# Down weights of units 2 to 7 fetched as whole words and split on chip, and the last two divisions later

## The chip, the cores and the metric

One core of a Trainium2 chip (trn2) runs the whole kernel in one launch; inputs and output are in HBM, all tensors FP32. The metric is the device time of one execution in microseconds. The engines are TensorE (PE in the profile; PEld is its weight load), VectorE (DVE), ScalarE (ACT), GpSimd (POOL) and SyncE (SP), which only issues transfers. POOL also issues some; those of SP and POOL run on the same 16 DMA engines.

## The reference

Linear attention over 8 batches x 8 heads (576 tokens, head size 64, 128 random features), and then a two-layer block on the 4608 tokens x 512 features that it gives.

```python
def phi(x):
    proj = np.einsum('bhsd,df->bhsf', x, w_phi)
    proj = proj - np.max(np.abs(proj), axis=-1, keepdims=True)
    return np.concatenate([np.exp(proj), np.exp(-proj)], axis=-1)
q_p, k_p = phi(q), phi(k)
kv, z = np.einsum('bhsf,bhsd->bhfd', k_p, v), np.sum(k_p, axis=2)
num = np.einsum('bhsf,bhfd->bhsd', q_p, kv)
den = np.einsum('bhsf,bhf->bhs', q_p, z)[..., None] + 1e-06
attn = num / den
...
h = x @ w_in
g = np.maximum(h, 0.0) + alpha * np.minimum(h, 0.0)
return g @ w_out
```

Here x is attn with heads side by side, w_in is 512 x 2048 and w_out 2048 x 512.

## The kernel before, in words

**Attention, 0 to about 320 us.** 32 pairs of heads are worked through one slot after another (`attention_units`); the table in `places` says at which slot each part of pair i comes. Near the end of a pair the denominator goes out to DRAM and comes back inverted and spread over partitions (`rec_out`, `spread`, L528 and L533), POOL multiplies the numerator by it (`finish`, L538: the division), and SP stores the product to `x_d` (L541). In between, the 64-bit weights are decoded to FP32 halves and stored twice: as whole words in `a_d` (256 columns per quarter, one word each), and as two parts, high and low, in `u_d` (up weights) and `v_d` (down weights). Every FP32 product is three matmuls: high x high, low x high, high x low (L584 to L586, L594 to L596, L876 to L878).

**Chunk 0, about 320 to 400 us.** The first 512 tokens go through the block plainly. The 2048 hidden features are 16 groups, ff = 0 to 15; two groups are a unit u. `up2` makes h of a group (12 matmuls), ACT and DVE turn it into g and split it (relu r, join g L265, cast gh, rest gl L152), and `down2` adds its product to the outputs po (12 matmuls, called d0 to d15 here). The order on PE is up 0 to 3, d0 to d3, up 4, up 5, then d4, up 6, d5, up 7 and so on to d13, up 15; then the first product of pair 1, d14, another product, d15. A slot of this order is U2 = 1/3 in the table's time, with t1 = 33.051 at d0. The weights come by SP: wa and ws for up, and `load_down` (L648) fetches wd of group ff + 4 when d of ff has been issued, so that d4 to d15 take theirs from `v_d`; the first four were kept on chip.

**Sums, beside chunk 0 and the first units.** The 4096 tokens that remain go as 4 pairs of chunks, by a scheme with 7 products in place of 8 that needs sums of weight quarters. `sums(u, down)` makes them: load the unit's whole words from `a_d` (POOL's queue, L713), two and then two more subtractions or additions (L720 to L727), split into high and low (halve on ACT L146, low on DVE L149), store to `us_d` or `vs_d` (POOL's queue, L741). They are needed for all 8 down units and all 8 up units; those of up units 3 to 7 are made just in time, in the units. SUMS lists them in order; the first NSUM = 9 (up and down of units 0 to 2, down of 3 to 5) are placed in chunk 0, one each 3 slots (SUM0, SUMD, with SUMT for the parts), the rest in the units of pair 1, in a `for` over u at the end. In chunk 0 the tiles of the sums come from rings: 3 for the loaded words, 4 for the split sums, so that a new split waits for an older store.

**Pair 1 and after.** `unit(p, u)` makes the 7 up products of a unit (6 matmuls each) into banks pa, pb, pc, and `down_pair` the down products.

PE, SP and POOL (and in attention ACT and DVE) follow the order of the table `todo`, sorted by time. From T2 on the order of ACT and DVE is set by the scheduler, in which `behind` keeps splits and sums behind the newest cast and rest. Each engine then works strictly in its order.

Of the kernel before, what the change touches and what calls it, by code (L numbers as in the profile page):

```python
# [26 lines left out]
NF = DFF // P  # L27
# [13 lines left out]
NPRE = 2  # L41
# [19 lines left out]
def places(i):  # L61
    early = True
    end = i >= NPAIR - 2
    lag = 0 if i >= NPAIR - 4 else 1
    first = {}
    if i == 0:
        first = dict(
            kz=0.5093, ka=0.6934, ko=0.8124, kr=1.1197, kc=1.4241,
            n=1.8361, q=(0.96, 0.9362, 0.4904), qe=(0.9994, 1.0, 0.8939),
        )  # L70
    if i == 1:
        first = dict(kz=0.0015, ka=0.0046, ko=0.0058)
    return dict(
        ld=-2.1 if i > 2 else -1.9,
        lv=-0.17 if i > 2 else -0.45,
        p=(-0.9955 if early else -0.997, -0.2197),
        pl=-0.219 if i > 2 else -0.2217,
        ke=(0.005, 0.008) if i > 2 else (-0.1643, -0.0202),
        kz=1.0035,
        ka=1.0012,  # L80
        ko=1.0045,
        kr=1.0191,
        kc=1.1461,
        q=(1.4089, 1.4543, 1.3558),
        qe=(1.4364, 1.4627, 1.3892),
        d=2.004,
        ds=2.0047,
        n=2.0062,
        s=2.1311,
        d9=2.025,  # L90
        dv=lag + 2.7686 if early else 2.842 if end else 2.7432,
        rd=lag + 2.82,
        rr=lag + 3.03 if lag else 3.06,
        x=lag + 3.72,
        xs=lag + 4.05 if lag else 3.851,
        y=0.0055,
        s0=2.007,
    ) | first
# [3 lines left out]
W0 = dict(load=-1.3, scale=-1.0712, split=-0.9512)  # L102
X0T = 5.52
X0L = 0.305
WDT = (33.2, 33.83, 33.86)
HEADS = (31.9, 32.3, 32.62, 32.9)
T2 = 33.05
HEAD = 4
# [1 line left out]
U2 = 1 / 3  # L110
# [1 line left out]
PAD = 32  # L112
GQ = (0.1093, 0.2682, 0.3222)
UPA = 2
SUM0, SUMD = 1.5, 3.0
SUMT = dict(load=-5.0, two=0.0, four=0.2, half0=0.6, half1=0.8, store0=1.5, store1=1.6)
SUMS = [(0, 0), (0, 1), (1, 0), (1, 1), (2, 0), (2, 1), (3, 1), (4, 1), (5, 1), (6, 1), (7, 1)]
NSUM = 9
NJIT = 3
XPT = (19.3, 19.301, 20.3, 21.3, 22.3, 31.7, 32.1, 32.4)  # L120
XP0, XPD = 6.6, 2.0
# [3 lines left out]
def fused_kernel(ctx: ExitStack, tc: tile.TileContext, kq, v, w_phi, w_in, w_out, alpha, out):  # L125
    nc = tc.nc
# [10 lines left out]
    def f(t):  # L137
        return t.bitcast(F32)
# [6 lines left out]
    def halve(dst, src):  # L145
        return act.activation(dst, src, AF.Copy, scale=0.5)  # L146

    def half_low(dst, src, hi):
        return dve.scalar_tensor_tensor(dst, src, 0.5, f(hi), op0=ALU.mult, op1=ALU.subtract)  # L149
# [79 lines left out]
    def decode_store(ff, z, o, n):  # L229
# [8 lines left out]
        load=decode_load,  # L238
# [14 lines left out]
    def behind(eng):  # L253
        return tc.issue_after(newest[eng].ins) if eng in newest and "pso" in late else ExitStack()
# [346 lines left out]
    xs, po = {}, {}  # L601
# [43 lines left out]
    def down_tile(name, dtype):  # L645
        return wdq.tile([P, 2, 2, WN], dtype, tag="wd", name=name, bufs=2 * NPRE)

    def load_down(ff):  # L648
        u, r = divmod(ff, 2)
        wd[ff] = down_tile(f"wd{ff}", F32R)  # L650
        nc.sync.dma_start(f(wd[ff]), v_d[u, :, 2 * r : 2 * r + 2])

    def load_up(p, u):
        if p:
# [42 lines left out]
    def sums(u, down):  # L697
# [13 lines left out]
        def load():  # L711
# [2 lines left out]
            st["b"] = [a[:, n] for n in ((0, 2, 1, 3) if down else (A11, A12, A21, A22))]  # L714
            st["src"] = (a[:, 0:2], a[:, 2:4]) if down else (a[:, 1:3], a[:, 0:4:3])

        def two():
            a11, a12, a21, a22 = st["b"]
            with behind("dve"):
                dve.tensor_tensor(a22, a21, a22, op=ALU.add)  # L720
                dve.tensor_tensor(a21, a11, a21, op=ALU.subtract)
# [7 lines left out]
        def half(n):  # L729
            a = st["src"][n]  # L730
            t = st[n] = new(n + 1).bitcast(F32R).rearrange("p (n t c) -> p n t c", t=2, c=WN)
            with behind("act"):
                halve(t[:, :, 0], a)
            with behind("dve"):
                half_low(t[:, :, 1], a, t[:, :, 0])
            if "hv" in late and not down:
                for j, s in enumerate(((S1, S2), (S3, S4))[n]):
                    wu[1, u, s] = t[:, j]
# [2 lines left out]
            pool.dma_start((us_d, vs_d)[down][u, :, 2 * n : 2 * n + 2], f(st[n]))  # L741

        parts = dict(load=load, two=two, four=four)
        parts |= {f"half{n}": lambda n=n: half(n) for n in range(2)}
        return parts | {f"store{n}": lambda n=n: store(n) for n in range(2)}

# [98 lines left out]
    for n, (k, ff) in enumerate(order):  # L845
        t = HEADS[n] if n < HEAD else t1 + (n - HEAD) * U2
        if k == "d":
            todo.append((t, lambda ff=ff: down2(ff)))
            if ff + 2 * NPRE < NF:
                todo.append((max(t + 0.0005, (WDT + (0,) * NF)[ff]), lambda ff=ff + 2 * NPRE: load_down(ff)))  # L850
            continue
        todo.append((t, lambda ff=ff: up2(0, ff)))
        if n >= HEAD and ff % 2 and ff // 2 + UPA < NU:
            todo.append((t + 0.0006, lambda u=ff // 2 + UPA: load_up(0, u)))
        for i, dt in enumerate(GH.get(ff, (0, *GQ))):
            todo.append((t + U2 - 0.01 + dt, lambda ff=ff, i=i: glu2(0, ff, i)))
    for u in range(NOWN, HEAD // 2 + UPA):
        todo.append((t1 + 0.0001 + 2.5 * U2 * (u > NOWN), lambda u=u: load_up(0, u)))
    work = [sums(*x) for x in SUMS] + [sums(u, 0) for u in range(NJIT, NU)]
    for n, parts in enumerate(work[:NSUM]):  # L860
        for k, dt in SUMT.items():
            todo.append((max(t1 + 0.0002, t1 + (SUM0 + SUMD * n + dt) * U2 + 0.002), parts[k]))
    for n, t in enumerate(XPT + tuple(t1 + (XP0 + XPD * n) * U2 + 0.003 for n in range(11))):
        todo.append((t, lambda n=n: (prep.extend(prepare(1) if n == 0 else []), pieces(1))))
    todo.append((t1 + 5 * U2, lambda: prep.pop(4)()))
# [279 lines left out]
```

## Time and profile before

| | |
|---|---|
| runs | 1002.67, 1003.82, 1003.88 us, median 1003.82 |
| profiled execution | 1001.65 us, span 999.9 us, granted clock 0.998 |
| PE matmul busy | 976.2 us (98%), 7200 instructions |
| DVE, ACT, POOL busy | 744.1 us (74%), 625.5 us (63%), 242.2 us (24%) |
| DMA | 258.52 MB, mean 259 GB/s |

The busy share is an average over stages with different limits. The page has a row of 40 slices for each engine, the DMA engines and the granted clock; views with a window show one stretch. A timeline gives, for each instruction, how long its engine was idle before it and who ended that; a view of waits sums this by pairs. Most rows of a helper (halve, low) have the helper's line, so tiles tell them apart: sv and su are tiles of sums of down and up weights, xo and xr inputs of pair 1 and later.

### The profile page before, as it was taken

The numbers are of one execution on the slowest core, as the hardware profiler recorded it, in microseconds if no ns is written. First come the engines' busy times: TensorE is split into PE (matmuls) and PEld (weight loads), VectorE is DVE, ScalarE is ACT, GpSimd is POOL, SyncE is SP. The second block draws the span as 40 slices with busy tenths as digits, with TensorE's granted clock in tenths as the row PEclk, the third lists the DMA queues.
The fourth block names the chain that finished last, engine by engine and source line by source line (L and its number), as shares of the span: only waits on it lengthen the run. The fifth ranks groups of instructions, "written<-read, shape, count | busy, mean of one in ns | idle before, by whom it ended". The sixth has DMA issues, their size and how long they took to land.

```text
span 999.9 us, 19129 instructions
## 1 busy us (share of the span) xinstructions
PE 976.2 (98%) x7200; PEld 789.5 (79%) x7200; DVE 744.1 (74%) x1174; ACT 625.5 (63%) x1224; POOL 242.2 (24%) x218
## 2 busy tenths in 40 slices
PE   8999999999999999899999999999999999999998
PEld 7666666666666877787888888888888888888887
DVE  6888888888885577687997465888366977565874
ACT  4799899899898234455566454665455655554553
POOL 1466676666665131121000000000000000000001
PEclk9999999999999999999999999999999999999999
DMA  5588889999885999996767566768567677565565
GB/s 180 186 297 289 301 300 310 313 316 328 310 278 195 333 352 417 378 330 215 275 215 276 183 238 204 273 209 275 202 208 250 234 238 265 169 221 192 185 221 182
DMA packets 99339, 258.52 MB, mean 259 GB/s; under 512 B 12656, under 2 KB 13296, under 8 KB 99248
## 3 DMA queue, kind: packets, MB, share of 16 engines
q1 hardware_dynamic: 88816, 221.71, 65.5%
q0 software_dynamic: 10000, 35.39, 9.2%
q8 instruction: 57, 0.93, 0.4%
q14 instruction: 34, 0.28, 0.1%
q10 hardware_dynamic: 432, 0.20, 0.1%
HBM read 196.16 MB, written 60.96 MB: 257 GB/s over the span
## 4 chain that ended last, share of the span: by engine, by line
PE 58%; DMA 9%; DVE 3%; issue 3%; ACT 1%; POOL 1%; SPq 0%; ACTq 0%; DVEq 0%; POOLq 0%
PE pa L876 5%; PE pa L878 5%; PE pa L877 5%; PE qa L878 5%; PE qa L877 5%; PE qa L876 5%; PE pc L876 3%; PE pc L877 3%; PE pc L878 3%; DMA xr<-x_d 2%; DMA sv<-a_d 2%; PE qc L878 2%; DMA vs_d<-sv 2%; PE qc L877 2%; PE qc L876 2%
## 5 line engine op out<-in xcount | busy, mean ns | idle before, releaser
L142 ACT CAST hv<-g 128x512 fp32r<-128x512 f32 x224 | 135.4, 618 | 80.8 <-PE qa L878 44.3
L152 DVE TENSOR_TENSOR hv<-g,hv 128x512 fp32r<-128x512 f32 x224 | 150.3, 685 | 40.4 <-ACT hv L142 39.1
L766 POOL DMA_DIRECT2D out_dram<-pt x35 | 19.0, 543 | 503.3 <-ACT pt L1044 419.0
L354 DVE TENSOR_REDUCE m<-pj 128x8 f32<-128x1024 f32 (+2 forms) x67 | 78.5, 1172 | 36.1 <-PE pj L350 36.1
L878 PE MATMUL qa<-hv,wv 128*128 128x512 f32 (+1 forms) x257 | 97.3, 379 | 0.1
L877 PE MATMUL qa<-hv,wv 128*128 128x512 f32 (+1 forms) x257 | 97.2, 378 | 0.0
L876 PE MATMUL qa<-hv,wv 128*128 128x512 f32 (+1 forms) x257 | 97.2, 378 | 0.0
L355 DVE TENSOR_TENSOR t<-pj,m 128x1024 f32<-128x1024 f32 (+2 forms) x67 | 78.8, 1177 | 4.4
L350 PE MATMUL pj<-w_sb,raw 64*128 64x128 f32 x1024 | 75.3, 287 | 4.1 <-DVE t L355 4.1
L350 PEld LDWEIGHTS pj<-w_sb,raw 64*128 64x128 f32 x1024 | 63.2, 189 | 19.5 <-issue 15.3
L377 POOL TENSOR_TENSOR y<-xk 128x1024 f32<-128x1024 f32 x30 | 71.0, 2368 | 5.2 <-ACT xk L369 5.2
L488 PE MATMUL n<-qf,sf 128*64 128x288 f32 x512 | 69.2, 412 | 0.0
L204 POOL TENSOR_TENSOR aw<-cw,aw 128x512 int32<-128x512 int32 x32 | 41.7, 1302 | 110.6 <-DVE aw L200 92.0
L369 ACT ACTIVATE xk<-t 128x1024 f32<-128x1024 f32 (+1 forms) x66 | 64.1, 1022 | 5.0 <-DVE t L355 5.0
L896 ACT ACTIVATE r<-g 128x512 f32<-128x512 f32 x65 | 37.4, 622 | 46.9 <-DVE g L892 46.8
L390 PE MATMUL kv<-xk,v 128*64 128x256 f32 x512 | 62.3, 385 | 0.0
L477 ACT ACTIVATE qf<-qt 128x512 f32<-128x512 f32 x116 | 60.8, 648 | 0.0
L142 ACT CAST xo<-xr 128x512 fp32r<-128x512 f32 x56 | 33.6, 619 | 43.4 <-DVE xr L819 21.9
L897 DVE SCALAR_TENSOR_TENSOR g<-r,al,g 128x512 f32<-128x512 f32 x65 | 45.9, 747 | 17.1 <-ACT r L896 16.9
L878 PEld LDWEIGHTS qa<-hv,wv 128*128 128x128 f32 x257 | 48.6, 189 | 7.3 <-DVE hv L152 0.5
L152 DVE TENSOR_TENSOR xo<-xr,xo 128x512 fp32r<-128x512 f32 x56 | 38.7, 701 | 20.8 <-ACT xo L142 20.4
L876 PEld LDWEIGHTS qa<-hv,wv 128*128 128x128 f32 x257 | 48.6, 189 | 6.9
(203 smaller groups left out, 2534.3 us busy)
## 6 DMA issues: line engine op xcount, KB each, us to landing
wv<-vs_d SPq DMA_DIRECT2D x64, 512.0 KB, 4.3
ws<-us_d SPq DMA_DIRECT2D x54, 512.0 KB, 3.8
wv<-v_d SPq DMA_DIRECT2D x48, 512.0 KB, 5.9
wa<-u_d SPq DMA_DIRECT2D x37, 512.0 KB, 5.5
raw<-kq_dram SPq DMA_DIRECT2D x31, 576.0 KB, 6.7
v<-v_dram SPq DMA_DIRECT2D x32, 320.0 KB, 5.1
rr<-rec_d SPq DMA_DIRECT2D x64, 144.0 KB, 3.8
x_d<-rr SPq DMA_DIRECT2D x32, 288.0 KB, 3.6
```

The lines of the kernel that those rows point to most:

```text
L142: return act.copy(dst, src)
L152: return eng.tensor_tensor(dst, src, f(hi), op=ALU.subtract)
L350: pe.matmul(dst[h, j], lhsT=c["raw"][hs, ts], rhs=w_sb[hs], start=True, stop=True)
L354: dve.tensor_reduce(m, src, axis=AX.X, op=ALU.max, apply_absolute_value=True)
L355: dve.tensor_tensor(t[:, hs, js], src, m.unsqueeze(3).broadcast_to([P, nh, nj, FD]), op=ALU.subtract)
L369: act.activation(x[:, a, :, js], c["t", 0][:, :, js], AF.Exp, scale=sg)
L377: pool.tensor_tensor(y, x[:, :, : 2 * FD], x[:, :, 2 * FD :], op=ALU.add)
L390: pe.matmul(c["kv"][h * D : (h + 1) * D, 0:2], lhsT=c["v"][:, tp, h, :], rhs=c["x", ch][:, :, h, j, :], start=tp == 0, stop=tp == NV - 1,)
L488: pe.matmul(ps[h * D : (h + 1) * D, :], lhsT=c["st"][:, a, h * D : (h + 1) * D], rhs=c["qf"][:, h, a, u * HS : (u + 1) * HS], start=a == 0 ...
L876: pe.matmul(ps, lhsT=wh, rhs=xh, start=first, stop=False, skip_group_check=True)
L877: pe.matmul(ps, lhsT=wl, rhs=xh, start=False, stop=False, skip_group_check=True)
L878: pe.matmul(ps, lhsT=wh, rhs=xl, start=False, stop=end, skip_group_check=True)
```

## The change

Three things. `load_down` is gone: `split_down` makes wd of groups 4 to 15 from the words of the sums' load, by a halve on ACT and a low on DVE for each group, in two new parts split0 and split1 of `sums`, ahead of the additions, which overwrite the words. The order of the sums follows: down units 2 to 7 each one to two slots before the d that needs its parts, up units 0 to 2 between, and down units 0 and 1, whose parts are on chip, in the units of pair 1. And for the last two pairs of heads the division and its store move from slot 3.72 and 3.851 to 6.75 and 6.76.

```diff
--- before.py
+++ after.py
@@ -91,8 +91,8 @@
         dv=lag + 2.7686 if early else 2.842 if end else 2.7432,
         rd=lag + 2.82,
         rr=lag + 3.03 if lag else 3.06,
-        x=lag + 3.72,
-        xs=lag + 4.05 if lag else 3.851,
+        x=lag + 3.72 if not end else 6.75,
+        xs=lag + 4.05 if lag else 6.76 if end else 3.851,
         y=0.0055,
         s0=2.007,
     ) | first
@@ -102,7 +102,6 @@
 W0 = dict(load=-1.3, scale=-1.0712, split=-0.9512)
 X0T = 5.52
 X0L = 0.305
-WDT = (33.2, 33.83, 33.86)
 HEADS = (31.9, 32.3, 32.62, 32.9)
 T2 = 33.05
 HEAD = 4
@@ -112,10 +111,10 @@
 PAD = 32
 GQ = (0.1093, 0.2682, 0.3222)
 UPA = 2
-SUM0, SUMD = 1.5, 3.0
-SUMT = dict(load=-5.0, two=0.0, four=0.2, half0=0.6, half1=0.8, store0=1.5, store1=1.6)
-SUMS = [(0, 0), (0, 1), (1, 0), (1, 1), (2, 0), (2, 1), (3, 1), (4, 1), (5, 1), (6, 1), (7, 1)]
-NSUM = 9
+SUMT = dict(load=-5.0, split0=-1.3, split1=-1.1, two=0.0, four=0.2, half0=0.6, half1=0.8, store0=1.5, store1=1.6)
+SUMS = {(2, 1): 5.4, (0, 0): 7.4, (3, 1): 9.4, (4, 1): 13.4, (1, 0): 15.4, (5, 1): 17.4, (6, 1): 21.4, (2, 0): 23.4, (7, 1): 25.4}
+NSUM = len(SUMS)
+SUMS |= {(u, 1): None for u in range(NPRE)}
 NJIT = 3
 XPT = (19.3, 19.301, 20.3, 21.3, 22.3, 31.7, 32.1, 32.4)
 XP0, XPD = 6.6, 2.0
@@ -645,10 +644,12 @@
     def down_tile(name, dtype):
         return wdq.tile([P, 2, 2, WN], dtype, tag="wd", name=name, bufs=2 * NPRE)
 
-    def load_down(ff):
-        u, r = divmod(ff, 2)
+    def split_down(ff, a):
         wd[ff] = down_tile(f"wd{ff}", F32R)
-        nc.sync.dma_start(f(wd[ff]), v_d[u, :, 2 * r : 2 * r + 2])
+        with behind("act"):
+            halve(wd[ff][:, :, 0], a)
+        with behind("dve"):
+            half_low(wd[ff][:, :, 1], a, wd[ff][:, :, 0])
 
     def load_up(p, u):
         if p:
@@ -714,6 +715,9 @@
             st["b"] = [a[:, n] for n in ((0, 2, 1, 3) if down else (A11, A12, A21, A22))]
             st["src"] = (a[:, 0:2], a[:, 2:4]) if down else (a[:, 1:3], a[:, 0:4:3])
 
+        def split(r):
+            split_down(2 * u + r, st["src"][r])
+
         def two():
             a11, a12, a21, a22 = st["b"]
             with behind("dve"):
@@ -741,6 +745,7 @@
             pool.dma_start((us_d, vs_d)[down][u, :, 2 * n : 2 * n + 2], f(st[n]))
 
         parts = dict(load=load, two=two, four=four)
+        parts |= {f"split{n}": lambda n=n: split(n) for n in range(2)}
         parts |= {f"half{n}": lambda n=n: half(n) for n in range(2)}
         return parts | {f"store{n}": lambda n=n: store(n) for n in range(2)}
 
@@ -846,8 +851,6 @@
         t = HEADS[n] if n < HEAD else t1 + (n - HEAD) * U2
         if k == "d":
             todo.append((t, lambda ff=ff: down2(ff)))
-            if ff + 2 * NPRE < NF:
-                todo.append((max(t + 0.0005, (WDT + (0,) * NF)[ff]), lambda ff=ff + 2 * NPRE: load_down(ff)))
             continue
         todo.append((t, lambda ff=ff: up2(0, ff)))
         if n >= HEAD and ff % 2 and ff // 2 + UPA < NU:
@@ -857,9 +860,10 @@
     for u in range(NOWN, HEAD // 2 + UPA):
         todo.append((t1 + 0.0001 + 2.5 * U2 * (u > NOWN), lambda u=u: load_up(0, u)))
     work = [sums(*x) for x in SUMS] + [sums(u, 0) for u in range(NJIT, NU)]
-    for n, parts in enumerate(work[:NSUM]):
+    for (x, t), parts in zip(SUMS.items(), work[:NSUM]):
         for k, dt in SUMT.items():
-            todo.append((max(t1 + 0.0002, t1 + (SUM0 + SUMD * n + dt) * U2 + 0.002), parts[k]))
+            if x[1] or "split" not in k:
+                todo.append((max(t1 + 0.0002, t1 + (t + dt) * U2 + 0.002), parts[k]))
     for n, t in enumerate(XPT + tuple(t1 + (XP0 + XPD * n) * U2 + 0.003 for n in range(11))):
         todo.append((t, lambda n=n: (prep.extend(prepare(1) if n == 0 else []), pieces(1))))
     todo.append((t1 + 5 * U2, lambda: prep.pop(4)()))
```

Line numbers of the changed kernel are up to 5 higher in these parts, and one lower above. On POOL, where the sums' loads begin (sv_0_0 is the loaded words of the down sums of unit 0, su of up sums, rr30 the division of pair 30), before:

```order
L713 DMA su_0_0_5210<-a_d_63 128x1024
L713 DMA sv_0_0_5212<-a_d_63 128x1024
L538 TENSOR_TENSOR rr30_5216<-s30_5024,rr30_5216 128x576
L713 DMA su_1_0_5277<-a_d_63 128x1024
L741 DMA us_d_60<-su_0_1_5264 128x1024
L741 DMA us_d_60<-su_0_2_5268 128x1024
L801 DMA xr1_1_5330<-x_d_57 128x1024
L538 TENSOR_TENSOR rr31_5294<-s31_5158,rr31_5294 128x576
L713 DMA sv_1_0_5346<-a_d_63 128x1024
L741 DMA vs_d_62<-sv_0_1_5337 128x1024
```

and now, behind the loads of sv_2_0, su_0_0 and sv_3_0, which open the list one after another:

```order
L806 DMA xr1_1_5310<-x_d_57 128x1024
L745 DMA vs_d_62<-sv_2_1_5340 128x1024
L745 DMA vs_d_62<-sv_2_2_5343 128x1024
L714 DMA sv_4_0_5402<-a_d_63 128x1024
L745 DMA us_d_60<-su_0_1_5388 128x1024
L745 DMA us_d_60<-su_0_2_5394 128x1024
L714 DMA su_1_0_5457<-a_d_63 128x1024
L745 DMA vs_d_62<-sv_3_1_5449 128x1024
L745 DMA vs_d_62<-sv_3_2_5452 128x1024
L537 TENSOR_TENSOR rr30_5212<-s30_5024,rr30_5212 128x576
L714 DMA sv_5_0_5506<-a_d_63 128x1024
L537 TENSOR_TENSOR rr31_5271<-s31_5158,rr31_5271 128x576
```

The two divisions have moved behind the stores of the sums of down unit 3, and behind five and six loads of words in place of two and three.

On ACT, from the last copy of attention to the cast of group 5 (r2_0_4 and gh2_0_4 are relu and cast of group 4, wd4 the high part of the down weights of group 4), before:

```order
L500 COPY s31_5158<-n31_1_5153 128x288
L146 ACTIVATE su_0_1_5264<-su_0_0_5210 128x2x256
L146 ACTIVATE su_0_2_5268<-su_0_0_5210 128x2x256
L146 ACTIVATE sv_0_1_5337<-sv_0_0_5212 128x2x256
L146 ACTIVATE sv_0_2_5342<-sv_0_0_5212 128x2x256
L261 ACTIVATE r2_0_4_5315<-h2_0_4_5298 128x512
L142 CAST gh2_0_4_5348<-g2_0_4_5340 128x512
L142 CAST xo1_7_0_5372<-xr1_0_3099 128x512
```

and now:

```order
L499 COPY s31_5158<-n31_1_5153 128x288
L145 ACTIVATE wd4_5287<-sv_2_0_5216 128x2x256
L145 ACTIVATE wd5_5290<-sv_2_0_5216 128x2x256
L260 ACTIVATE r2_0_4_5295<-h2_0_4_5274 128x512
L141 CAST gh2_0_4_5322<-g2_0_4_5316 128x512
L145 ACTIVATE sv_2_1_5340<-sv_2_0_5216 128x2x256
L145 ACTIVATE sv_2_2_5343<-sv_2_0_5216 128x2x256
L141 CAST xo1_7_0_5348<-xr1_0_3099 128x512
```

Two splits stand ahead of the relu of group 4 where four stood, and two that stood there come behind its cast.

On DVE, at the fourth unit of pair 1 (g_1_3_1 with pa1_3 is the last reader of bank pa of unit 3, g_1_4_11 with pa1_4 reads the third product of unit 4), before:

```order
L897 SCALAR_TENSOR_TENSOR g_1_3_1_6207<-r22_1_3_6259,al1_82,g_1_3_1_6207 128x512
L727 TENSOR_TENSOR su_6_0_6187<-su_6_0_6187 128x256
L149 SCALAR_TENSOR_TENSOR su_5_2_6323<-su_5_0_6103,su_5_2_6323 128x2x256
L892 TENSOR_TENSOR g_1_4_11_6295<-pa1_4_6240,p5_1_4_6314 128x512
L897 SCALAR_TENSOR_TENSOR g_1_3_1_6207<-r21_1_3_6268,al1_82,pa1_3_6156 128x512
L720 TENSOR_TENSOR su_7_0_6273<-su_7_0_6273 128x256
```

and now:

```order
L901 SCALAR_TENSOR_TENSOR g_1_3_0_6218<-r12_1_3_6268,al1_82,g_1_3_0_6218 128x512
L901 SCALAR_TENSOR_TENSOR g_1_3_1_6219<-r22_1_3_6271,al1_82,g_1_3_1_6219 128x512
L724 TENSOR_TENSOR su_7_0_6285<-su_7_0_6285 128x256
L901 SCALAR_TENSOR_TENSOR g_1_3_1_6219<-r21_1_3_6280,al1_82,pa1_3_6168 128x512
L725 TENSOR_TENSOR su_7_0_6285<-su_7_0_6285 128x256
L896 TENSOR_TENSOR g_1_4_11_6307<-pa1_4_6252,p5_1_4_6326 128x512
L148 SCALAR_TENSOR_TENSOR su_5_2_6335<-su_5_0_6115,su_5_2_6335 128x2x256
```

The two readers have changed places. On PE one thing moves: the first product of pair 1 (6 matmuls) stands behind up 14, where it stood behind up 15. On SP the twelve wd loads are gone and the two stores to x_d stand behind the wa and ws loads of units 5 and 6.

## Rows read from the trace of the kernel before

**Rows 1.** PE in chunk 0: start, length us, engine, line, operation, tiles, [idle before].

```profile
323.75 0.48 PE L594 MATMUL po<-own_x,wd 128*128 128x512 f32 x1
...
340.98 0.48 PE L594 MATMUL po<-gh,wd 128*128 128x512 f32 x1 [1.43 <-ACT gh L142]
...
353.42 0.48 PE L596 MATMUL po<-gl,wd 128*128 128x512 f32 x1 [1.08 <-DVE gl L152]
...
395.40 0.38 PE L584 MATMUL h<-x0cp,ws 128*128 128x512 f32 x1
...
397.77 0.38 PE L586 MATMUL h<-x0pt,ws 128*128 128x512 f32 x1
...
403.68 0.38 PE L594 MATMUL po<-gh,wd 128*128 128x512 f32 x1
```

**Rows 2.** PE in the first units of pair 1, same view.

```profile
421.02 0.48 PE L876 MATMUL pa<-xo,ws 128*128 128x512 f32 x1 [2.54 <-ACT u L888]
...
432.07 0.48 PE L876 MATMUL pa<-xo,ws 128*128 128x512 f32 x1 [1.71 <-ACT u L888]
...
453.65 0.48 PE L876 MATMUL pa<-xo,wa 128*128 128x512 f32 x1 [1.89 <-DVE g L897]
...
458.03 0.38 PE L876 MATMUL pa<-xo,wb 128*128 128x512 f32 x1
```

**Rows 3.** Windows: us; PE, PEld, DVE, ACT, POOL busy; PEclk, DMA, GB/s.

```profile
339.50:402.60 63.10, 58.13 (x261) 48.41 (x260) 46.10 (x82) 26.65 (x47) 12.56 (x22) 1.00 0.99 377
...
455.00:456.00 1.00, 1.00 (x3) 0.80 (x3) 1.00 (x3) 0.12 (x1) 0.00 (x0) 0.50 0.09 33
```

**Rows 4.** Waits of ACT, 339 to 403: us in all, times, longest.

```profile
ACT sv L146 <- DMA vs_d<-sv: 7.5, 3, 3.6
```

**Rows 5.** Waits of DVE, 339 to 403.

```profile
DVE sv L149 <- ACT sv L146: 4.6, 6, 1.2
...
DVE su L149 <- ACT su L146: 3.3, 3, 1.6
...
DVE gl L152 <- ACT gh L142: 3.1, 5, 0.7
```

**Rows 6.** DMA issues, 300 to 460: count, KB, median us to landing.

```profile
wd<-v_d SPq DMA_DIRECT2D x12, 512.0 KB, 11.9
```

**Rows 7.** Timeline of ACT ahead of the first stall.

```profile
338.26 0.63 ACT L146 ACTIVATE sv<-sv 128x512 fp32r<-128x512 f32 x1 [1.94 <-DMA v_d<-raww]
338.80 0.58 ACT L261 ACTIVATE r<-h 128x512 f32<-128x512 f32 x1
```

**Rows 8.** Timeline of DVE, five successive rows, end of chunk 0.

```profile
395.77 0.74 DVE L265 SCALAR_TENSOR_TENSOR g<-r,al,h 128x512 f32<-128x512 f32 x1
396.43 0.42 DVE L726 TENSOR_TENSOR sv<-sv 128x256 f32<-128x256 f32 x1
396.88 0.43 DVE L727 TENSOR_TENSOR sv<-sv 128x256 f32<-128x256 f32 x1
397.23 0.69 DVE L152 TENSOR_TENSOR gl<-g,gh 128x512 fp32r<-128x512 f32 x1
397.83 0.69 DVE L819 TENSOR_TENSOR xr<-xr 128x512 f32<-128x512 f32 x1
```

**Rows 9.** Timelines of POOL, then DVE, at the second division.

```profile
350.81 1.41 POOL L538 TENSOR_TENSOR rr<-s,rr 128x576 f32<-128x576 f32 x1 [11.79 <-DMA rr<-rec_d]
...
350.92 1.85 DVE L149 SCALAR_TENSOR_TENSOR su<-su,su 128x512 fp32r<-128x512 f32 x1 [0.40 <-ACT su L146]
```

**Rows 10.** Timelines in the units: POOL, DVE, ACT, DVE.

```profile
408.30 1.06 POOL L713 DMA_DIRECT2D sv<-a_d  x2
...
415.05 0.43 DVE L720 TENSOR_TENSOR sv<-sv 128x256 f32<-128x256 f32 x1 [3.55 <-DMA sv<-a_d]
...
427.23 0.63 ACT L146 ACTIVATE sv<-sv 128x512 fp32r<-128x512 f32 x1 [2.74 <-DMA vs_d<-sv]
...
452.86 0.74 DVE L897 SCALAR_TENSOR_TENSOR g<-r,al,pa 128x512 f32<-128x512 f32 x1
```

## The prediction

> **What bounds the kernel now.** I began with the page's busy shares: TensorE (PE) works 98% of the span, so whatever can be won is idle PE time. The slices put it in two places: the start, which the change does not touch, and 325 to 460 us. There I read PE's own timeline. PE issues a matmul every (397.77 - 395.40) / 11 = 0.2155 us when nothing holds it [rows 1]. Chunk 0's down product d0 starts at 323.75 and d15 at 403.68. Between them lie 336 matmuls (26 groups of 12, then 6, 12 and 6), so an unheld PE would start d15 at 323.75 + 336 x 0.2155 = 396.2: **7.5 us are lost**. The idle times beside 340.98 and 353.42 name ScalarE's (ACT) cast gh and VectorE's (DVE) rest gl; three more of the same kind follow.
>
> From d15 to 458.03 (the last product of unit 4 of pair 1) there are 210 matmuls, or 45.3 us, and it took 54.4: **9.1 us are lost** [rows 1, 2]. Three waits make 6.1 of it (2.54, 1.71, 1.89). After the third the granted clock fell to 0.50, the lower level of 1.2 GHz [rows 3]: from 453.65 to 458.03 PE did 12 matmuls in 4.38 us instead of 2.59, which costs 1.8. The rest is slow restarts.
>
> Then I asked what made ACT and DVE late, since neither is full: from 339.5 to 402.6 DVE is busy 46.1 of 63.1 us, idle 17.0 [rows 3]. Both take their instructions strictly in order. ACT waited 7.5 us for stores of finished sums (vs_d) to free their tiles [rows 4], and while it stood, DVE waited for it: 4.6 and 3.3 us before the low halves of the sums, 3.1 before gl [rows 5]. The DMA engines are the root: their share is 0.99 in this stretch at 377 GB/s, and twelve wd loads of 512 KB take a median 11.9 us to land [rows 3, 6]. The first stall shows the pattern: ACT stood 1.94 us for v_d<-raww to land, and only then came the relu of h_4, which PE had long finished [rows 7].
>
> **The change, part by part.**
> *Twelve wd loads go* from SP's queue: 12 x 0.524 = 6.3 MB, at the stretch's 377 GB/s some 17 us of DMA work in 63. SP loses twelve waits for PE and two for the divisions' data; the wa and ws loads behind them come sooner. By itself this is worth next to nothing on PE, whose waits in chunk 0 name ACT and DVE and not these loads; what it buys is early stores and loads for ACT and DVE. No load is added: the a_d words of units 2 to 7 were fetched before too, for the sums.
>
> *Twelve halves on ACT and twelve lows on DVE come in.* ACT has room (26.7 of 63.1 us busy [rows 3]; 12 x 0.63 = 7.6 more). DVE is the question. Its rows succeed each other at 0.66 us (join g), 0.60 (128x512 rows) and 0.35 or 0.45 (128x256 sums) [rows 8]. From the join of h_4 to gl_15 the changed order has 102 DVE rows: 12 joins, 58 of 128x512 (12 gl, 11 xo, 7 xr, 18 lows of sums, 10 of the new lows; the first two come earlier) and 32 of 128x256. Work: 12 x 0.66 + 58 x 0.60 + 32 x 0.40 = 55.5 us. Before it was 80 rows and 43.5 us; of the 12.0 us added, 6.0 are the ten new lows, and 6.0 are sums, which now start later and so fall into this stretch.
>
> *The last two divisions* leave their place ahead of the sums' loads on POOL, where POOL stood for their rec_d data, 11.8 us for the second alone [rows 9]; with them go two x_d stores on SP that waited behind. Nothing needs these tokens before pair 4. Moved is not removed: at 350.81 a division of 1.41 us ran on POOL, and the DVE row that started at 350.92 took 1.85 us where a row of that shape takes 0.69 [rows 8], so the division cost DVE 1.16 [rows 9]; gl_6 and PE's stall at 353.42 followed. I charge 2 x 1.16 = 2.3 us to DVE, now near gl_8 and gl_9. The Trainium skill, page "SBUF — State Buffer", section "Who interferes with whom", says a DVE instruction with two SBUF inputs and a GpSimd instruction that reads SBUF exclude each other for a whole instruction, and its summary advises keeping the loser off the critical path. That speaks against this part, which sets both divisions where DVE is fullest; by that rule they would cost at most 1.41 each, 2.8 in all, and the sum would be 0.5 us worse.
>
> *Sum of chunk 0.* h_4 is complete at 323.75 + 60 x 0.2155 = 336.7, the relu takes 0.58 [rows 7], so the join starts near 337.5. To the start of gl_15: 55.5 - 0.6 + 2.3 = 57.2 us of work. DVE's idle time I set at 4 us: the 3.1 before gl stays (it waits for a cast that needs the join), 1 for the rest; the 7.9 before the sums' lows came mostly of ACT standing at stores, and I take them as gone. The ends are 0 and the whole 17.0. gl_15 then starts at 337.5 + 57.2 + 4 = 398.7, and d15, which needs it 0.4 us in, at 399.0: **4.7 us** earlier than 403.68. With idle 0 PE itself sets 396.2 and the gain is 7.5. The chunk thus turns from waiting for DMA into waiting for DVE.
>
> *Units of pair 1.* The wait at 421.02 goes back to sums loads issued at 408.30, for which DVE stood 3.55 us until 415.05; the one at 432.07 to ACT standing 2.74 us, until 427.23, for a store of those sums [rows 10]. The loads are issued right behind the last store of chunk 0, which I put at 399, nine us sooner, while d15 moves only 4.7: they gain about four and a half us on PE and wait in front of no one. The wait at 453.65 is one of order: unit 5's first product takes over a bank whose last reader is the DVE row at 452.86, listed behind the row that needs the product PE did just before the wait. In the changed order that reader stands ahead of it, so PE need not wait. All 9.1 could go. But DVE now has no slack: a unit with sums costs it 2 x 0.60 + 4 x 0.66 + 4 x 0.40 + 2 x 0.60 = 6.6 us, and unit 3 adds two hv lows and four differences, 3.6: 10.2 against PE's 42 x 0.2155 = 9.05. I keep 1.2 us for that and 1.8 for a clock fall behind it, 3.0 together (ends 0 and 9.1): **6.1 us** gained.
>
> The sum is 10.8 us: 1001.65 - 10.8 = 990.9 against the profiled execution. The median of the runs shown is 2.2 us above that execution, so my forecast is 1003.8 - 10.8 = **993.0 us**. After 460 us I change nothing: PE is full there, and orders are the same but for neighbours that change places.
>
> **The rivals.**
> *Everything goes.* Should DVE keep up (its idle falls to nearly 0), both losses vanish: 7.5 + 9.1 = 16.6, or 987.2. For it speaks that ACT has half its time free; against it the 10.2 us in unit 3 and the divisions.
> *Units keep their losses.* If the first two sums of the unit stage still arrive late, or new stalls of DVE fall on other banks, with the clock following as at 453.65, only chunk 0 gains: 4.7, or 999.1. For it: the 10.2 us in unit 3, and DVE's order there is as tight as before. Against it: the two rows that changed places.
> *DVE becomes a worse bound than DMA was: slower.* Place: DVE's list in chunk 0, whose head always stands for an ACT row behind other ACT rows. If its idle stays 17.0, gl_15 starts at 337.5 + 57.2 + 17 = 411.7, d15 at 412.0, 8.3 late; the sums' loads move with it, and of the units only the third wait and its clock fall (1.9 + 1.8) are won: 1003.8 + 8.3 - 3.7 = 1008.4. It decides from an idle of 12.4 us up. Against it: most of that idle has a DMA behind it, and there is a quarter less to move.
> *A load in the new place is late.* d4 now hangs on POOL's first load, issued as d0 starts (323.75), instead of an SP load. Its two halves on ACT must be done when h_4 is, at 336.7, so it has 11.7 us to land. Even the 11.9 us that the wd loads took in the median with the DMA engines full would cost d4 about 1.5; but later units have the same dependence, and if each of the six loses 1.8 us, the 10.8 are gone: no change, 1003.8. Against it: those medians belong to the full DMA engines that the change relieves, and the loads of units 3 to 7 are issued four or more groups of 2.59 us ahead.
>
> **How the numbers follow.** The forecast has 0.55, everything gone 0.12, units unchanged 0.18, slower 0.08, no change 0.07. What a measurement of this kernel can tell from no change is about 0.2%, 2 us. The first three are faster, 0.85, of which I move 0.01 to slower: 0.84, 0.07, 0.09. The range 988.0 to 1000.5 takes in the forecast with an idle from 0 to 9 us, what lies between it and the first rival, and the second; out are the slower case, no change and the very best.
>
> **What would show it.** Right: no wd<-v_d load and 252 MB in the page's total instead of 258.5; DMA share below 0.9 from 335 to 400; ACT waits for vs_d stores near 0; DVE busy above 90% in that stretch; d15 near 399; no PE wait behind the row that frees unit 3's bank; the clock at 1.00 through 460. Wrong: DVE idle over 12 us in chunk 0, PE waits of over 2 us before gl anywhere but near d8 to d10, or a stall in units 0 to 5 longer than 2 us.

## The result, and the profile after

The changed kernel ran at a median of **989.1 us** (988.12 to 990.01, 4 runs), the kernel before beside it at 1003.85 (1002.67 to 1006.69); the ratio is 0.985, 95% interval 0.983 to 0.987. Run again with others on one chip it gave 990.3 against 1002.6, a ratio of 0.987 (0.985 to 0.989). So 12 to 15 us were won where 10.8 were forecast, and the time lies in the range near its fast end. By the first comparison it is nearer to the rival "everything goes" (987.2) than to the forecast of 993.0, by the second nearer to the forecast. The two profiled executions differ by 11.7 (1001.65 and 990.01); the rest of the first 14.7 is spread between runs.

PE's timeline after, as in [rows 1, 2]: the first row of d0, the wait in d8, the first row of d15 and its wait, the one named wait in the units, the first product of unit 5, and A22 of unit 4.

```profile
324.26 0.48 PE L593 MATMUL po<-own_x,wd 128*128 128x512 f32 x1
...
362.25 0.48 PE L595 MATMUL po<-gl,wd 128*128 128x512 f32 x1 [0.94 <-DVE gl L151]
...
398.19 0.44 PE L593 MATMUL po<-gh,wd 128*128 128x512 f32 x1
...
399.29 0.48 PE L595 MATMUL po<-gl,wd 128*128 128x512 f32 x1 [0.45 <-DVE gl L151]
...
432.65 0.48 PE L880 MATMUL pa<-xo,su 128*128 128x512 f32 x1 [0.77 <-ACT u L892]
...
443.15 0.48 PE L880 MATMUL pa<-xo,wa 128*128 128x512 f32 x1
...
445.84 0.38 PE L880 MATMUL pa<-xo,wb 128*128 128x512 f32 x1
```

From d0 to d15 chunk 0 took 73.93 us where 336 unheld matmuls take 72.4: 1.5 us lost, where it was 7.5 [rows 1]. From d15 to A22 of unit 4 it took 47.65 instead of 45.3: 2.4 lost, where it was 9.1 [rows 2]. Together 12.7 of the 16.6 are won; 0.5 of that is given back ahead of d0, which starts later in this execution, and 0.5 after 460 us.

The windows of the changed kernel, columns as in [rows 3]:

```profile
338.00:398.00 60.00, 59.06 (x274) 51.21 (x272) 55.84 (x101) 35.05 (x64) 15.06 (x25) 1.00 0.92 339
400.00:460.00 60.00, 59.20 (x272) 50.80 (x272) 49.38 (x90) 36.67 (x65) 12.80 (x25) 1.00 0.88 313
```

DVE is now busy 93% of chunk 0, DMA's share is 0.92 at 339 GB/s where it was 0.99 at 377, and the granted clock stays at 1.00, the 2.4 GHz level, through all 60 us of the units. ACT's 7.5 us for stores of sums [rows 4] are 1.0 in the same stretch.

The divisions in their new place, on POOL and then on DVE, as in [rows 9]:

```profile
358.23 1.43 POOL L537 TENSOR_TENSOR rr<-s,rr 128x576 f32<-128x576 f32 x1
359.60 0.60 POOL L714 DMA_DIRECT2D sv<-a_d  x1
360.22 1.42 POOL L537 TENSOR_TENSOR rr<-s,rr 128x576 f32<-128x576 f32 x1
```

```profile
359.33 2.86 DVE L151 TENSOR_TENSOR gl<-g,gh 128x512 fp32r<-128x512 f32 x1 [0.69 <-ACT gh L141]
```

POOL waits for nothing in front of them any more. But one row of DVE, the gl that d8 waits for, takes 2.86 us where its like takes 0.69: 2.17 us more, and ends 0.55 us behind the second division. PE's wait of 0.94 at 362.25 is the price. By the rows the first division ends at 359.66, 0.33 us into this one; what held it from there until the second began at 360.22, while POOL issued a load, they don't show.

### The profile page after: what moved, and what is told of

Read it like the earlier page. It is cut to its first block, busy times and chain, and to the rows that moved or that the text cites. A ratio compares the mean times of both kernels' runs of the same rounds, so it can differ in the third digit from the quotient of the medians.

```text
span 988.2 us, 19123 instructions
## 1 busy us (share of the span) xinstructions
PE 973.3 (98%) x7200; PEld 790.1 (80%) x7200; DVE 748.3 (76%) x1186; ACT 632.6 (64%) x1236; POOL 241.8 (24%) x218
## 4 chain that ended last, share of the span: by engine, by line
PE 74%; DVE 5%; DMA 4%; issue 2%; ACT 2%; POOL 0%; SPq 0%; DVEq 0%; ACTq 0%; POOLq 0%
PE pa L880 5%; PE pa L882 5%; PE pa L881 5%; PE qa L882 5%; PE qa L881 5%; PE qa L880 5%; PE kv L389 4%; PE n L487 4%; PE pj L349 4%; PE pc L881 3%; PE pc L882 3%; PE pc L880 3%; PE qc L882 2%; PE qc L881 2%; PE qc L880 2%; PE d L506 2%
## 5 line engine op out<-in xcount | busy, mean ns | idle before, releaser
L882 PEld LDWEIGHTS qa<-hv,wv 128*128 128x128 f32 x257 | 48.6, 189 | 6.9
L880 PEld LDWEIGHTS qa<-hv,wv 128*128 128x128 f32 x257 | 48.6, 189 | 6.9
L881 PEld LDWEIGHTS qa<-hv,wv 128*128 128x128 f32 x257 | 48.6, 189 | 6.8
```

Source lines behind the costliest of these rows:

```text
L880: pe.matmul(ps, lhsT=wh, rhs=xh, start=first, stop=False, skip_group_check=True)
L881: pe.matmul(ps, lhsT=wl, rhs=xh, start=False, stop=False, skip_group_check=True)
L882: pe.matmul(ps, lhsT=wh, rhs=xl, start=False, stop=end, skip_group_check=True)
```

## The experiments

My theory was that the twelve wd loads filled the DMA engines, and that the rest followed. The rivals were the new order of the sums and the place of the divisions. For every profiled execution the table gives PE's loss in chunk 0 (d0 to d15, above 72.4 us) and in the units (d15 to the first product of unit 6, 240 matmuls, above 51.7 us), beside the ratio to the kernel before on the same chip.

| kernel | wd loads | ratio (95%) | chunk 0 | units |
|---|---|---|---|---|
| before | yes | 1 | 7.5 | 9.1 |
| changed | no | 0.985 (0.983 to 0.987) | 1.5 | 2.4 |
| changed, again | no | 0.987 (0.985 to 0.989) | 2.2 | 1.7 |
| order_only | yes | 0.996 (0.995 to 0.998) | 11.6 | 2.4 |
| loads_back | yes | 0.989 (0.987 to 0.991) | 6.5 | 1.8 |
| before_no_loads | no | 0.989 (0.987 to 0.991) | 5.4 | 2.0 |
| after_no_split | no | 0.985 (0.983 to 0.987) | 0.3 | 1.2 |
| div_only | yes | 0.992 (0.991 to 0.994) | 7.1 | 1.5 |
| div_back | no | 0.990 (0.988 to 0.991) | 3.2 | 4.8 |
| div_early | no | 0.989 (0.987 to 0.990) | 3.2 | 2.3 |
| div_split | no | 0.990 (0.988 to 0.992) | 3.0 | 3.6 |
| store_later | yes | 0.990 (0.988 to 0.992) | 3.0 | 3.3 |
| junk_loads | as bytes | 0.999 (0.997 to 1.000) | 10.1 | 5.6 |
| su_early | no | 0.989 (0.987 to 0.990) | 3.4 | 3.1 |

Three things to keep in mind with this table. Each loss is read from one execution: the two of the changed kernel differ by 0.7 us in either column, and over all rows d0 starts between 323.1 and 326.7 and the part behind the units varies by 3.1 us, so the losses don't add up to the times. In loads_back and order_only the profiled execution is the slowest of its runs (997.2 and 1002.0). And a fall of the granted clock to 0.50 behind a wait is counted in: in chunk 0 of order_only, loads_back, div_only and junk_loads, in the units of before, div_back and junk_loads.

**loads_back**

```diff
...
+            if ff + 2 * NPRE < NF:
+                todo.append((max(t + 0.0005, (WDT + (0,) * NF)[ff]), lambda ff=ff + 2 * NPRE: load_down(ff)))
...
-            if x[1] or "split" not in k:
+            if "split" not in k:
```

> The changed kernel with the twelve wd loads of 512 KB back on SP's queue in their old places, and without the new halves and lows; the new order of the sums and the moved divisions stay. If the traffic was the cause (my theory), the DMA share from 338 to 398 goes back to about 0.99, ACT stands at stores of sums again (several us of vs_d<-sv), and chunk 0 loses again most of its 6 us; the bank order of the units keeps its 3.7 us: 996 to 1001 us. If the new order of the sums or the place of the divisions was the cause, the loads change little: 988 to 992, and below the changed kernel's 989.1 if the DVE work that goes was the limit.

Measured: 993.7 us (991.04 to 997.17), between both ranges. My theory asked for more: against the changed kernel only 4.6 us come back, from kernels of two chips. The DMA share is 1.02 (this view can pass 1) at 399 GB/s from 338 to 398, more than before, and yet ACT's waits for vs_d stores in that stretch are 0.3 us in all, where I expected several, and the units lose only 1.8. Most of the 6.5 in chunk 0 is one wait of PE for a load, at the first product of pair 1, with a granted clock of 0.50 behind it from 399 to 402:

```profile
397.76 0.48 PE L888 MATMUL pa<-xo,wa 128*128 128x512 f32 x1 [2.79 <-DMA wa<-u_d]
```

The loads of wa, on SP between the wd loads, land after a median 14.1 us from 323 to 400, where the changed kernel has 6.1. So the wd loads cost something in the new order too, but by way of other loads and not of ACT's stores.

**order_only**: the same, with the divisions in their old place too.

```diff
-        x=lag + 3.72 if not end else 6.75,
-        xs=lag + 4.05 if lag else 6.76 if end else 3.851,
+        x=lag + 3.72,
+        xs=lag + 4.05 if lag else 3.851,
```

> The kernel before with the new order of the sums alone: twelve wd loads on SP, divisions in their old place. Traffic as the cause: 997 to 1004 us, since nothing relieves the DMA engines. Order as the cause: 989 to 993. Divisions as the cause (POOL standing for their data ahead of the sums' loads): about 1000 to 1004, with POOL idle 10 us or more before the second division.

Measured: 999.9 us (998.88 to 1001.96). Between the source of this kernel and that of loads_back lies only the place of the divisions, and it is worth 6.2 us on one chip. POOL, ACT and PE show how:

```profile
337.64 1.40 POOL L538 TENSOR_TENSOR rr<-s,rr 128x576 f32<-128x576 f32 x1 [9.80 <-DMA rr<-rec_d]
338.99 0.60 POOL L720 DMA_DIRECT2D su<-a_d  x1
339.59 0.53 POOL L720 DMA_DIRECT2D sv<-a_d  x1
...
354.60 1.68 POOL L538 TENSOR_TENSOR rr<-s,rr 128x576 f32<-128x576 f32 x1 [13.96 <-DMA rr<-rec_d]
```

```profile
362.42 0.63 ACT L146 ACTIVATE sv<-sv 128x512 fp32r<-128x512 f32 x1 [7.06 <-DMA vs_d<-sv]
```

```profile
366.24 0.80 PE L594 MATMUL po<-gh,wd 128*128 128x512 f32 x1 [7.90 <-ACT gh L142]
```

POOL stands 9.8 and 14.0 us for the divisions' data, the second and third load of the sums go out only at 339 and the first store only behind 356; ACT stands 7.1 us for that store, and in the end PE stands 7.9 us in one place. So the divisions were no mere cost to move; this rival was right.

**before_no_loads**: d4 to d15 multiply by the weights of units 0 and 1.

```diff
...
-        wd[ff] = down_tile(f"wd{ff}", F32R)
-        nc.sync.dma_start(f(wd[ff]), v_d[u, :, 2 * r : 2 * r + 2])
+        wd[ff] = wd[ff % (2 * NPRE)]
```

> The kernel before without the twelve wd loads and with nothing in their place: d4 to d15 multiply by the weights of units 0 and 1 that are there already, so the output lacks the down weights of units 2 to 7 in chunk 0. Order of sums and divisions as before. Traffic as the cause: DMA share near 0.85 from 339 to 402, d15 starts at 397 to 399 where it was 403.68, time 993 to 998. Order or divisions as the cause: d15 stays later than 402, time 1001 to 1004.

Measured: 993.1 us (989.03 to 994.19), 11 us faster, as the traffic theory had it. But d15 starts at 402.54, 77.8 us after d0: chunk 0 wins 2.1, the units 7.1, and the DMA share from 339 to 402 is 0.93 and not 0.85. POOL still stands 10.0 and 7.0 us for the divisions' data. The time came out, its place did not.

**after_no_split**: the same replacement in the changed kernel, for the twelve new halves and lows.

> The changed kernel without the twelve new halves and twelve new lows: d4 to d15 multiply by the weights of units 0 and 1, so the output lacks the down weights of units 2 to 7 in chunk 0. ACT loses 7.6 us of work and DVE 7.2 in chunk 0. If DVE is the limit that is left there (my theory), the waits before gl near d8 and d15 (0.94 and 0.45 us) shrink and the time is 987 to 988.5. If the splits cost nothing because PE is the limit, 988.5 to 990 like the changed kernel.

Measured: 988.1 us (985.98 to 992.37); against the changed kernel that can't be told apart by time. By its trace, one execution, PE loses 0.3 us in chunk 0 instead of 1.5 and 2.2, and the waits before gl at d8 and d15 are gone. This speaks for the splits on ACT and DVE as what is left of the loss in chunk 0, as my theory had it.

**div_only**: the kernel before with the two lines of order_only's diff the other way round.

> The kernel before with the two divisions and their x_d stores moved, nothing else. With the new order of the sums already there, the same move was worth 6.2 us (999.9 to 993.7). If it pays because POOL no longer stands 10 us and more for data ahead of the sums' loads, it pays here too: 996 to 999. If it pays only with the new order, which has the first loads where they can use it: 1002 to 1004.

Measured: 994.5 us (993.86 to 996.12) against 1002.3 on this chip: 7.8 us, with all loads in place, and faster than either range. Chunk 0 wins hardly anything (7.1, with a wait of 2.75 us at d4 and a clock of 0.50 behind it), the units nearly everything (1.5).

**div_back**: the changed kernel with the divisions in their old place.

> The changed kernel with the two divisions and their x_d stores back in their old place. If the divisions hurt only as long as full DMA engines bring their data late, they hurt little here, and the d8 wait of 0.94 us that they cause in the new place goes: 988 to 991. If POOL standing in front of the sums' loads is a cost of its own, as with the twelve loads there, about 6 us come back: 994 to 996.

Measured: 991.7 us (991.48 to 992.92), in the gap between both ranges. Chunk 0 loses 3.2 and the units 4.8, of which a part follows a wait of 2.06 us in the units, after which the granted clock falls to 0.50.

**div_early** and **div_split** try to win the d8 wait. In both the first division goes where POOL is idle; in div_split the second goes behind the last store of chunk 0.

```diff
-        x=lag + 3.72 if not end else 6.75,
-        xs=lag + 4.05 if lag else 6.76 if end else 3.851,
+        x=5.29 if i == NPAIR - 2 else 6.75 if end else lag + 3.72,
+        xs=5.3 if i == NPAIR - 2 else 6.76 if end else lag + 4.05 if lag else 3.851,
```

(div_split has 11.06 and 14.0 for the second.)

> The changed kernel with the first of the two divisions put between the first loads of the sums and the first store of them on POOL, where POOL is idle from 327 to 341 and DVE has 3.6 us idle before its first join; the second stays. If a division costs DVE a good 1.1 us and DVE is the limit of chunk 0, d8 waits less than 0.3 us instead of 0.94 and d15 starts 0.5 to 1.1 us sooner: 988 to 988.7. If PE is the limit: no difference, 989 to 990.

> As the run before, and the second division behind the last store of chunk 0 on POOL, ahead of the loads of the first two sums of pair 1. If DVE is the limit, chunk 0 gains 1 to 1.5 us against the changed kernel; the loads behind the division come 1.4 us later and may cost units 0 and 1 up to as much: 987.5 to 989.5. If PE is the limit and the loads are late: 989.5 to 991.

Measured: 990.7 us (990.4 to 992.6) and 991.4 (990.02 to 994.42), both above the ranges for a limit of DVE. No gain in either. In div_early the wait in d8 is gone, as expected, and d15 waits instead, for ACT. The first row of its d15:

```profile
398.69 0.48 PE L593 MATMUL po<-gh,wd 128*128 128x512 f32 x1 [0.85 <-ACT gh L141]
```

A stall of under 1 us that is taken away at d8 is met again at d15, where no division stands: there the lists of ACT and DVE set the end. That they did so in the changed kernel as well was not tested.

**after_again**

> The changed kernel once more, unedited, so that the other three of this group are compared with it on one chip: ratio to the kernel before 0.983 to 0.989, as in its first runs.

Measured: 990.3 us (988.39 to 991.42). The gain holds on a second chip.

**junk_loads**: the changed kernel with the old bytes on SP's queue, for nobody.

```diff
+    def junk(ff):
+        u, r = divmod(ff, 2)
+        nc.sync.dma_start(junk_d[ff], v_d[u, :, 2 * r : 2 * r + 2])
...
```

> The changed kernel with twelve transfers of 512 KB from v_d to a scratch tensor in DRAM on SP's queue, at the old places of the wd loads; nothing reads what they write. With the real loads in place of the new halves and lows it was 4.6 us slower. If the bytes on the DMA engines were the cause: 993 to 997. If it was what the loads made wait (SP's queue behind a wd tile that is not free, d rows behind a late load), which these transfers do not do: 989 to 991.

Measured: 1002.1 us (1000.82 to 1004.69), slower than either theory gave it: the whole gain is gone. The DMA issues of the changed kernel, 323 to 400 us, and those of junk_loads (columns as in [rows 6]):

```profile
wa<-u_d SPq DMA_DIRECT2D x7, 512.0 KB, 6.1
sv<-a_d POOLq DMA_DIRECT2D x6, 512.0 KB, 10.2
```

```profile
junk_d<-v_d SPq DMA_DIRECT2D x12, 512.0 KB, 19.9
...
wa<-u_d SPq DMA_DIRECT2D x7, 512.0 KB, 15.0
sv<-a_d POOLq DMA_DIRECT2D x6, 512.0 KB, 11.0
```

The loads of wa, which share SP with the junk, land after 15.0 us instead of 6.1, and PE stands 4.69 us before d12, as its first row shows:

```profile
388.46 0.79 PE L593 MATMUL po<-gh,wd 128*128 128x512 f32 x1 [4.69 <-ACT wd L145]
```

This wait can't be booked to the bytes, though. The load behind that split was issued at 368.13 and had landed at 381.03. ACT came to the split only at 387.79, because here it stands behind the cast of group 13:

```profile
385.28 0.62 ACT L141 CAST gh<-g 128x512 fp32r<-128x512 f32 x1 [0.30 <-DVE g L264]
387.26 0.62 ACT L141 CAST xo<-xr 128x512 fp32r<-128x512 f32 x1 [1.36 <-DVE xr L830]
387.79 1.15 ACT L145 ACTIVATE wd<-sv 128x512 fp32r<-128x512 f32 x2
```

In the changed kernel the same split, at 378.71, stands ahead of the cast of group 12. So the order of ACT's rows changed with the junk. The wait and the clock of 0.50 that goes with it (386 to 392; d12 and the 12 matmuls behind it take 7.6 us instead of 5.2) make 7.1 of the 10.1 us of chunk 0. The run shows that such bytes make other loads late. What they cost PE by themselves it does not show; they also go from DRAM to DRAM and wait for no tile, which the wd loads don't.

**store_later**: the kernel before with one number changed, the place of the x_d stores of the last four pairs on SP.

```diff
-        xs=lag + 4.05 if lag else 3.851,
+        xs=lag + 4.05 if lag else 4.2,
```

> The kernel before with the x_d stores of the last four pairs a third of a slot later on SP, nothing else: loads and divisions stay, but the planner writes ACT's and DVE's rows from chunk 0 on in another order, with the reader of unit 3's bank ahead of the reader of unit 4's. If that swap of readers is worth what I gave it (1.9 us of wait and 1.8 of clock fall) and the rest of the new order is worth nothing: 999 to 1001. If the orders are worth nothing: 1002 to 1005. If a new order of ACT and DVE is itself worth as much as loads or divisions: below 997 or above 1006.

Measured: **992.8 us** (990.11 to 995.07), a gain of 9.8 us on the chip where the whole change gains 12.3, with every wd load and both divisions in place. This is the run that I had expected least. SP in the kernel before, and then in this one:

```profile
336.91 0.32 SPq L541 DMA_DIRECT2D x_d<-rr  x1
337.28 0.93 SPq L651 DMA_DIRECT2D wd<-v_d  x2
338.44 2.03 SPq L533 DMA_DIRECT2D rr<-rec_d  x2
...
341.27 0.54 SPq L663 DMA_DIRECT2D ws<-u_d  x1
352.24 0.32 SPq L541 DMA_DIRECT2D x_d<-rr  x1
352.66 0.89 SPq L651 DMA_DIRECT2D wd<-v_d  x2
353.60 0.43 SPq L663 DMA_DIRECT2D wa<-u_d  x1
```

```profile
333.40 1.97 SPq L651 DMA_DIRECT2D wd<-v_d  x3
338.87 1.09 SPq L533 DMA_DIRECT2D rr<-rec_d  x2
340.06 0.66 SPq L541 DMA_DIRECT2D x_d<-rr  x1
...
341.44 0.58 SPq L663 DMA_DIRECT2D ws<-u_d  x1
344.64 0.32 SPq L651 DMA_DIRECT2D wd<-v_d  x1
348.40 0.32 SPq L541 DMA_DIRECT2D x_d<-rr  x1
349.82 0.32 SPq L651 DMA_DIRECT2D wd<-v_d  x1
350.19 0.56 SPq L663 DMA_DIRECT2D wa<-u_d  x1
```

In the kernel before, SP issues nothing from 341.8 to 352.2: the x_d store at its head waits for the second division, which on POOL waits 11.8 us for its data [rows 9]. Both queues stand for the same rec_d data, and behind SP's head wait two wd loads that in the other run go at 344.6 and 349.8. The store ahead of it, of the first division, held SP as well: two wd loads went out at 337.3, just ahead of the loads of the second division's data, where store_later sends them off by 335.4. Those data loads are issued at 338.4 and 338.9 in the two runs, but the second division starts at 350.8 in the one and 346.5 in the other. I take it that they stood behind the wd loads; no run separates that. The windows of the kernel before and of store_later show what the DMA engines did meanwhile:

```profile
336.00:360.00 24.00, 21.46 (x98) 17.84 (x97) 15.54 (x24) 9.41 (x17) 8.13 (x13) 1.00 0.92 320
352.00:358.00 6.00, 4.92 (x23) 4.05 (x22) 4.61 (x7) 1.74 (x3) 3.92 (x8) 1.00 0.74 213
```

```profile
336.00:360.00 24.00, 22.72 (x105) 19.30 (x104) 18.45 (x31) 11.00 (x19) 7.95 (x13) 1.00 1.03 406
352.00:358.00 6.00, 6.00 (x29) 5.29 (x28) 4.01 (x7) 2.66 (x5) 0.07 (x1) 1.00 1.02 415
338.00:398.00 60.00, 58.72 (x272) 50.89 (x271) 46.49 (x81) 28.37 (x49) 13.28 (x23) 1.00 1.03 414
```

320 GB/s against 406: in 24 us the kernel before moves 2.1 MB less, about 5 us of work at 414 GB/s, and that backlog then sits in front of the stores that ACT waits for. More than half of it is missing from 352 to 358 (213 GB/s against 415): while the queues stand, the transfers issued earlier still run (394 GB/s from 344 to 352), and when these are done the engines are in part idle. In store_later the DMA engines are fuller than before (1.03), PE loses 3.0 us in chunk 0 instead of 7.5, and ACT has no wait for a vs_d store at all.

One thing stays open here. ACT's and DVE's rows are put in order by a planner, and this edit changed that too: by the tile names in the traces at least 54 of DVE's rows stand elsewhere, and on POOL the loads of the next sums stand ahead of the last store instead of behind it. How much of the 9.8 us is the free queue and how much the new order was not separated. The same holds for every edit above: read this way, at least 46 of DVE's rows moved in before_no_loads, 57 in div_only, 42 in junk_loads, 35 between order_only and loads_back and 13 in div_back. Only the changed kernel run again has the same rows in the same order. So the single gains are what an edit won with its new order, and no more.

**su_early**: the changed kernel with the second sum at 5.6 instead of 7.4.

> The changed kernel with the second sum, (0, 0), at 5.6 instead of 7.4: its four sums on DVE stand among those of the first, ahead of the join of h_4, where DVE was idle for 3.57 us. If DVE is the limit of chunk 0, its work there starts 1.7 us earlier, and d8 and d15 wait less: 0.5 to 1.3 us faster than the changed kernel on the same chip. If the su words land too late for that place, the sums of the first stand behind them and the join of h_4 is late: slower by up to 1 us.

Measured: 991.9 us (991.2 to 992.68) against 990.3 on one chip: 1.6 slower, which the intervals of the two ratios don't separate. The four sums did go ahead of the first join, but two us_d stores now stand on POOL ahead of the next load of a sum, as the first rows show, and ACT waits 13.0 us for such loads from 324 to 400 us, as the second fence shows, where it waited 7.0 in the changed kernel.

```profile
343.03 1.13 POOL L745 DMA_DIRECT2D us_d<-su  x2
344.15 0.53 POOL L714 DMA_DIRECT2D sv<-a_d  x1
```

```profile
ACT wd L145 <- DMA sv<-a_d: 13.0, 3, 5.9
```

No version was measurably faster than the changed kernel.

## Why the prediction held, and where its steps failed

**Where the idle time was** held: both stretches, 7.5 and 9.1 us, gave nearly all of the gain. So did most of the signs: no wd load, 252.2 MB, DVE busy 93%, ACT's stores near 0, no wait at unit 5's first product, the clock at 1.00. The DMA share was to fall below 0.9 from 335 to 400; it was 0.90, and 0.91 in the second execution.

**The term of chunk 0** was 4.7 and measured 6.0 and 5.4. Its working was close: the first join at 338.15 instead of 337.5, gl_15 at 398.55 instead of 398.7, with d0 0.5 later than before. "The chunk thus turns from waiting for DMA into waiting for DVE" agrees with after_no_split, in whose chunk 0 only 0.3 us are lost.

**The term of the units** was 6.1 and measured 6.7 and 7.4. The 1.8 us for a clock fall did not come due: no stall of these units was followed by one. The reason I gave for the third wait fell in part. The reader of unit 3's bank stands ahead in store_later too, and there unit 5's first product is not held. But the same wait comes one unit later, 1.73 us at unit 6's first product, behind DVE rows that follow each other without a gap. So the swap alone only moved the wait. In the changed kernel it comes at neither place; I put that down to a DVE that is on time, which was not tested.

**"The DMA engines are the root"** failed as a step. I read a share of 0.99 over 63 us as a full resource. In 24 us at its start they moved 320 GB/s, and with the same bytes and 406 GB/s PE lost 6.3 us instead of 16.6 in the two stretches (store_later). Nor did the chain from full engines to late stores to ACT come back with the wd loads: in loads_back the share is 1.02 and ACT waits 0.3 us for vs_d stores where it waited 7.5. The loads are a cost (before_no_loads, and in loads_back the wait for wa), but the edits that freed the heads of two queues without taking away a byte won as much as 7.8 and 9.8 us, the planner's new orders included.

**The divisions** I costed at 2.3 us of DVE and nothing gained. The price came out: 2.17 us on one DVE row. The Trainium skill, page "SBUF — State Buffer", section "Who interferes with whom", says that a DVE instruction with two SBUF inputs and a GpSimd instruction that reads SBUF hold each other off for a whole instruction. The trace agrees in part: the row that started at 359.33 ends 0.55 us behind the second division, but it was there before that division, and from the end of the first at 359.66 to 360.22 nothing in this rule holds it. The sign of the sum was wrong: div_only wins 7.8 us, and 6.2 lie between order_only and loads_back. I had the fact in hand, "x_d stores on SP that waited behind", and gave it no number.

**The parts don't add.** Taking away the loads wins 11.0 us, moving the divisions 7.8, moving the stores 9.8, the new order of the sums 4.2; the whole change wins 12 to 15. I read this as one chain (late loads, then late stores, then ACT, DVE and PE) that each cuts at another link, so that what is won by one can't be won again by the next. The forecast came out because it was made from the stretches' losses and a new limit, not from the parts. It was luck as far as the root goes: the sum asked only how much of the waiting would go, and most of it went, whether by the loads that I named or by the free queues that I gave nothing.

**Rivals.** "Everything goes" (987.2) came near: 12.7 of 16.6 went. "Units keep their losses" fell, with 2.4 of 9.1 left there. Slower and no change had their conditions tested: DVE's idle time stayed at 4 us of 60, and in the changed kernel no wait of PE names a split of wd. One sum there was wrong: a load that lands after 11.9 us instead of 11.7 makes the relu of group 4 late by 0.2 us, not d4 by 1.5.

## What to carry to other kernels

Before a busy DMA share is called the limit, look at what the head of each queue waits for: a store that waits for a late division blocks every load behind it on its queue, and idle engines now are full engines later. When an edit can shift a planner's order, run one tiny edit as a control; here moving a few stores won four fifths of the whole on the same chip. And read each wait down to its last link: the wait of junk_loads looked like a late load and was a late place in a list. Remedies that cut one chain at different links don't add, so forecast from the lost time and the next limit.

## What was not expected of the hardware

Twelve transfers from DRAM to DRAM of 512 KB took a median 19.9 us to land, where wd loads of that size into the chip took 11.9 [rows 6]. Of PE's waits in the units, 1.89 us (before), 2.06 (div_back) and 2.23 (junk_loads) were each followed by a granted clock of 0.50, and 1.73 us (store_later, order_only) were not; but the 2.54 us at 421.02 [rows 2] were not either, with 1.00 in the window behind it. In chunk 0, 2.75 us (div_only) and 2.79 (loads_back) were, and 2.73 (before_no_loads) was not. So the length of the wait alone does not decide.
